# Linear attention and a squared-ReLU layer: the second batch's place around the end of the weight conversion, and strip two's second product by two Strassen steps

## The chip, the cores and the metric

The kernel runs on one core of a Trainium2 chip, as one launch. The metric is the device time of that launch in microseconds; lower is better. The engines are TensorE (PE, with its weight loads shown as PEld), VectorE (DVE), ScalarE (ACT), GpSimd (POOL) and SyncE (SP), which here issues nearly all transfers on one queue, in program order.

## The reference

Eight batches of eight heads, 576 rows, 64 features, all in float32; the two weight matrices come as float64.

```python
kv = np.einsum('bhsd,bhse->bhde', k, v)
out = np.einsum('bhsd,bhde->bhse', q, kv)
rms = np.sqrt(np.mean(out * out, axis=-1, keepdims=True) + 1e-06)
x = (out / rms * g_norm)          # then (B,H,S,D) -> (4608, 512)
h = x @ w_in                      # 512 x 2048
r = np.maximum(h, 0.0)
return ((r * r) @ w_out)          # 2048 x 512
```

## The kernel before

**Strips.** The 4608 token rows are 36 tiles of 128; four tiles make a strip of 512 rows, and there are nine strips (`s` = 0 to 8; "strip one" is `s` = 0). Each strip has a first product (x times w_in, squared ReLU) and a second one (times w_out). The list `steps` holds first the calls of one, then of the other, and the loop at the end of the kernel calls them in order; all scheduling is by hand, so every engine gets its instructions in program order.

**Products.** Strip one's first product is plain (`up_first`, 16 steps, L609), since the weights are still being converted. In all later strips it is a Winograd-Strassen product with seven block products (`up`, L573). The second product of a strip with `s < DEEP` is by one such step: `down`, seven block products `p`, each in two halves `i`, with 128x256 matmuls at L573; strip one takes them in the order 1, 2, 5, 6, 7, 3, 4. From `s = DEEP` on it is by two steps: `down_deep`, 49 small products with 128x128 matmuls at L758 (`small_products`), whose operand sums are `leaf_sums` and whose results `together` adds on DVE. A float32 matmul shows as two records. `combine` takes a finished block out of PSUM: a copy by ACT (`snap`, L583) or an addition by DVE (`o_sb`, L711). `sums_g` adds two quarters of the activations for product 5, and `sums_in(g)` forms the Winograd sums of w_in for group g, after ACT has scaled them (L252); `sums_x(s)` forms those of x.

**Weights.** The float64 words come as 32 raw pieces of 0.5 MB (`load_piece`, tag `raw`, eight buffers), are converted two at a time by ACT (L205, L208) and DVE (L217 to L226), and DVE forms the sums of w_out and stores them in DRAM (`w_out`, from tiles `wt` that share the raw buffers). `convert(n)` runs ahead of the steps of strip one's first product, and a new piece is loaded when a buffer comes free. Three of the seven w_out operands (`w_first`) stay in SBUF for strip one. For the two-step product each w_out operand needs four more sums: `deep_sums(p, w)`, four DVE subtractions (L243) into a tile `w_t`, stored to `w_deep` in strip `DEEP - 1`. Blocks are fetched by `stream()`, in the order of `to_stream`, into four buffers that `w_t` shares:

```python
t = deep[p] = stream_pool.tile([P, 4, FQ // 2, P], FP32, name="w_t", tag="w_blk")
minus(nc.vector, t[:, 0], b12, b11)
...
t = stream_pool.tile([P, 4, FQ // 2, P], FP32, name="w_blk", tag="w_blk")
```

**Attention.** A batch has four pairs of heads (b, p). `load` fetches a pair's q, k and v (0.8 MB), `load_rest` and `load_q_rest` the last 64 rows of a batch. The work is cut into `slices`: per pair a transposition of q (T) and the key/value product (K, L352), then per two tiles `query` (L383), `normalized` and `features` (L470, transposed into xT). `attend(n)` runs the slices up to number n; the loop calls it after every step. K of a pair also issues the load of a later pair. In strip one the eight T and K slices of batch two (b = 1) stand behind the last eight steps of the first product, one each, and its queries behind the first six steps of the second product; pairs (1,0) and (1,1) and the rest rows are loaded at steps 2 and 4.

Of the kernel before, what the change touches and what calls it, by code (L numbers as in the profile page):

```python
# [10 lines left out]
FP32 = mybir.dt.float32  # L11
# [9 lines left out]
def kernel(  # L21
# [34 lines left out]
    nc = tc.nc  # L56
    P = 128
# [4 lines left out]
    NP = H // 2  # L62
    FC = d_ff // P
    C = S // P
# [5 lines left out]
    STRIP = NT * P  # L70
    TH = STRIP // 2
    N_STRIP = N_TILE // NT
    DEEP = 2
    SQ = 32
    Q_ON_PE = 2
    X_ON_PE = 2
# [8 lines left out]
    small = ctx.enter_context(tc.tile_pool(name="small", bufs=3))  # L85
    g_pool = ctx.enter_context(tc.tile_pool(name="g", bufs=4))
    dram = ctx.enter_context(tc.tile_pool(name="dram", bufs=1, space=bass.MemoryType.DRAM))
    conv = ExitStack()
    raw_pool = conv.enter_context(tc.tile_pool(name="raw", bufs=8))
    wtmp = conv.enter_context(tc.tile_pool(name="wtmp", bufs=4))  # L90
    apsum = ctx.enter_context(tc.tile_pool(name="apsum", bufs=2, space=bass.MemoryType.PSUM))
    fpsum = ctx.enter_context(tc.tile_pool(name="fpsum", bufs=1, space=bass.MemoryType.PSUM))
# [5 lines left out]
    def load(b, p, q_eng):  # L98
        hs = slice(2 * p, 2 * p + 2)
        inputs = (("q", q, q_eng), ("k", k, nc.sync), ("v", v, nc.sync))  # L100
        if b == 0 and p >= 2:

            h_place = g_pool.tile([P, 4, C * P], FP32, name="first_qkv", tag="gt")
        for i, (n, src, eng) in enumerate(inputs if b == 0 else inputs[1:] + inputs[:1]):
            whole = src[b, hs, 0 : C * P].rearrange("h (sp c) d -> sp h c d", c=C)
            if n == "q" and b >= Q_ON_PE:

                t = qkv_pool.tile([P, 4 * C, SQ], FP32, name=n, tag=n)
                for a in range(4):
                    h, f = divmod(a * SQ, D)  # L110
                    eng.dma_start(
                        out=t[ts(a, SQ)],
                        in_=src[b, 2 * p + h, 0 : C * P, f : f + SQ].rearrange("(i k) f -> i k f", k=4 * C),
                    )
            elif n != "q":
                if b == 0 and p >= 2:
                    t = h_place[:, i].rearrange("p (h c d) -> p h c d", h=2, c=C)
                else:
                    t = qkv_pool.tile([P, 2, C, D], FP32, name=n, tag=n)
                eng.dma_start(out=t, in_=whole)  # L120
            else:

                if b == 0 and p >= 2:
                    t = h_place[:, i].rearrange("p (c h d) -> p c h d", h=2, c=C)
                else:
                    t = qkv_pool.tile([P, C, 2, D], FP32, name=n, tag=n)
                for h in range(2):
                    eng.dma_start(out=t[:, :, h, :], in_=whole[:, h])
            main[n, b, p] = t
# [47 lines left out]
    w_out = dram.tile([7, P, 2, FQ, P], FP32, name="w_out")  # L177

    w_deep = dram.tile([7, P, 4, FQ // 2, P], FP32, name="w_deep")
# [314 lines left out]
    def sums_x(s):  # L494
        xc[s] = t1, t2, t3, t4 = [
            sum_pool.tile([P, TH // SQ, KH, SQ], FP32, name=f"x_t{i}", tag="sum") for i in range(4)
        ]
        x = lambda kh, th: halves(s, kh, th)
        minus(nc.vector, t1, x(0, 1), x(0, 0))
        minus(nc.vector, t2, x(1, 1), t1)  # L500
        minus(nc.vector, t3, x(1, 1), x(0, 1))
        minus(nc.vector, t4, x(1, 0), t2)

    slices, ready = [], {}
# [23 lines left out]
    def attend(n):  # L528
        while slice_at[0] < min(n, len(slices)):
            fn, a = slices[slice_at[0]]  # L530
            fn(*a)
            slice_at[0] += 1
# [145 lines left out]
    def down(s, p, i):  # L678
        if i == 0:
            open_bank(p)  # L680
        a = {1: 11, 2: 21, 6: 11, 7: 12, 3: 21, 4: 22}.get(p)
        w = w_blk[s, p]
        product(
            p, i,
            lambda fc: (gq[s, 1, fc // 2][:, fc % 2] if p == 5 else gq[s, a][:, fc])[:, ts(i, P)],
            lambda fc: w[:, :, fc], FQ,
        )
        if i == 0:
            if s == DEEP - 1:
                deep_sums(p, w)  # L690
            return
        del w_blk[s, p]
        if s == 0 and p in (6, 7, 3) or s == DEEP - 1 and p not in (3, 4):
            stream()
        if s == DEEP - 1:
            nc.sync.dma_start(out=w_deep[B_OUT[p]], in_=deep.pop(p))

        if p == (1 if s else 2):
            for g in range(NG):
                x = gq[s, 11][:, ts(g, 2)]  # L700
                minus(nc.vector, x, gq[s, 1, g], x)
        if p == (2 if s else 5):
            minus(nc.vector, gq[s, 21], gq[s, 21], gq[s, 11])

        def store(th, eh):
            def f(b, a=None):
                o = out_tile()
                if a is None:
                    nc.scalar.copy(o, b)
                else:  # L710
                    nc.vector.tensor_tensor(out=o, in0=b, in1=a, op=ALU.add)  # L711
                send(s, th, eh, o)
            return f

        combine(p, store(0, 0), store(0, 1), store(1, 0), store(1, 1))
# [4 lines left out]
    def deep_sums(p, w):  # L720
        t = deep[p] = stream_pool.tile([P, 4, FQ // 2, P], FP32, name="w_t", tag="w_blk")
        b11, b12, b21, b22 = (w[:, e, ts(f, FQ // 2)] for f in range(2) for e in (1, 0))
        minus(nc.vector, t[:, 0], b12, b11)
        minus(nc.vector, t[:, 1], b22, t[:, 0])
        minus(nc.vector, t[:, 2], b22, b12)
        minus(nc.vector, t[:, 3], b21, t[:, 1])
# [98 lines left out]
    for s in range(N_STRIP):  # L825
        attend(ready[s])
        if s == 0:
            steps = [(2, up_first, (g, fh, i)) for g in range(NG) for fh in range(2) for i in range(2)]
        else:
            steps = [(1, up, (s, g, p)) for g in range(NG) for p in ORDER]  # L830
        n_up = len(steps)
        if s < DEEP:

            steps += [(2, down, (s, p, i)) for p in (ORDER if s else (1, 2, 5, 6, 7, 3, 4)) for i in range(2)]
        else:
            steps += [(2, down_deep, (s, k, i)) for k in range(7) for i in range(2)]
        goal = ready.get(s + 1, len(slices))
        total, done = sum(w for w, _, _ in steps), 0
        for i, (w, fn, a) in enumerate(steps):
            if s == 0 and i < n_up:  # L840

                convert(5 + (3 * i + 2) // 4)
                if i in (2, 4):
                    load_next()
                if i == 2:
                    load_q_rest(0, nc.sync)
                    load_rest(1, nc.sync)
                    load_q_rest(1, nc.sync)
            elif s == 0 and i == n_up:
                convert(len(conversions))  # L850
                conv.close()
                sum_pool = ctx.enter_context(tc.tile_pool(name="sum", bufs=8, reuse_waits="tile"))
                c_pool = ctx.enter_context(tc.tile_pool(name="c", bufs=6, reuse_waits="tile"))
                stream_pool = ctx.enter_context(tc.tile_pool(name="stream", bufs=4, reuse_waits="tile"))
                stream(3)
                for b, t in enumerate(w_first):
                    for e in range(2):
                        nc.sync.dma_start(out=w_out[b, :, e], in_=t[:, :, ts(e, P)])
            if s == 0 and n_up <= i < n_up + NG:
                sums_g(0, i - n_up)  # L860
            fn(*a)
            done += w
            if s:
                attend(ready[s] + int((goal - ready[s]) * min(done / (0.42 * total), 1)))
                if s >= DEEP and i == n_up - 3:
                    leaf_sums(s, 4)
                if s == DEEP - 1 and i == len(steps) - 1:
                    sums_x(s + 1)
                    stream(4)
                continue  # L870
            if i in (n_up + 4, n_up + 5):
                load_next()
            if i == n_up + 6:
                load_rest(2, nc.sync)
                load_q_rest(2, nc.sync)
            if i - n_up in (7, 9, 11, 13):
                sums_in((i - n_up - 7) // 2)
            if i == n_up + 9:
                sums_x(1)

            n_kv = ready[0] + 2 * NP
            if i < n_up:
                attend(ready[0] + max(0, (i + 1) - n_up + 2 * NP))
            else:
                attend(n_kv + (goal - n_kv) * min(i + 1 - n_up, 6) // 6)


# [28 lines left out]
```

## Time and profile before

| | |
|---|---|
| median of 7 runs | 945.17 us (942.43 to 946.65) |
| the profiled execution | 945.19 us, of which the span is 943.4 |
| busy: PE, PEld, DVE, ACT | 916.0, 805.4, 658.3, 227.1 us |
| mean granted TensorE clock | 0.995 of full speed |
| HBM read, written | 153.62 MB, 31.20 MB |

The span is the part of the execution that the profile shows. PE's busy time is the sum of its matmul records, so what is left of the span is time in which TensorE waits. "Busy time by stage" gives, for a stretch of the span, its length and each engine's busy time with the number of instructions, then the granted clock, the mean busy share of the sixteen DMA engines and GB/s. In the views in order of time a bracket at a line's end holds the engine's idle time before that line and what ended it.

### The profile page before, as it was taken

To read this page: it belongs to the slowest core of one execution; us is meant where nothing else is said; L and a number is where in the kernel's file an instruction comes from. 1 tells how busy PE (TensorE), PEld (TensorE's weight loads), DVE (VectorE), ACT (ScalarE), POOL (GpSimd) and SP (SyncE) were. 2 spreads that over 40 slices of the span, in tenths; PEclk is the share of its full clock that TensorE was granted. 3 is DMA by queue.
4 is the path that set the end of the run, shared out by engine and by line. 5 is a ranking of instruction groups with operands and counts; after the bars stand their busy time and mean duration, and the time that the engine had idled before them with its cause. 6 is when DMAs were issued, how large, how long until landed. Compare 5 with 4: busy or idle time off the path is not lost.

```text
span 943.4 us, 17026 instructions
## 1 busy us (share of the span) xinstructions
PE 916.0 (97%) x6880; PEld 805.4 (85%) x6880; DVE 658.3 (70%) x1147; ACT 227.1 (24%) x494; POOL 1.7 (0%) x7
## 2 busy tenths in 40 slices
PE   5899899999999999999999999999999999999998
PEld 4444787888888998899989998899889988998898
DVE  4998845586436996489737975698559854983496
ACT  4797432320023102210222013200320022002200
POOL 0000000000000000000000000000000000000000
PEclk9999999999999999999999999999999999999999
DMA  9799783537875585648664874477516831682075
GB/s 277 246 276 302 251 244 129 132 94 261 299 235 143 165 301 200 151 146 290 218 153 114 312 244 134 108 282 253 161 44 232 302 99 60 224 302 66 1 259 177
DMA packets 164286, 185.94 MB, mean 197 GB/s; under 512 B 83952, under 2 KB 137712, under 8 KB 155632
## 3 DMA queue, kind: packets, MB, share of 16 engines
q1 hardware_dynamic: 163888, 184.72, 61.4%
q8 instruction: 54, 0.88, 0.4%
q10 hardware_dynamic: 320, 0.13, 0.1%
q14 instruction: 24, 0.20, 0.1%
HBM read 153.62 MB, written 31.20 MB: 196 GB/s over the span
## 4 chain that ended last, share of the span: by engine, by line
PE 89%; DMA 5%; DVE 4%; ACT 1%; issue 1%; SPq 0%; DVEq 0%; ACTq 0%
PE ps_A L573 29%; PE ps_B L758 18%; PE ps_B L573 14%; PE ps_A L758 14%; PE ps_C L573 7%; PE x_ps L383 2%; PE kv_ps L352 2%; DMA raw<-in_moe_w_out_dram 2%; PE ps_A L609 2%; DMA x_d<-x_q 1%; DMA k_rest<-in_k_dram 1%; PE ps_B L609 1%; DVE w_c L223 1%; DMA raw<-in_moe_w_in_dram 1%; DMA v<-in_v_dram 0%
## 5 line engine op out<-in xcount | busy, mean ns | idle before, releaser
L573 PE MATMUL ps_A<-x_t,w_in 128*128 128x256 f32 x768 | 183.2, 381 | 0.0
L573 PEld LDWEIGHTS ps_A<-x_t,w_in 128*128 128x128 f32 x768 | 144.4, 190 | 20.3 <-ACT snap L583 0.3
L758 PE MATMUL ps_B<-w_blk,g_s 128*128 128x128 f32 x896 | 109.2, 275 | 0.0
L758 PEld LDWEIGHTS ps_B<-w_blk,g_s 128*128 128x128 f32 x896 | 104.6, 192 | 0.0
L758 PE MATMUL ps_B<-w_blk,gt 128*128 128x128 f32 x672 | 84.2, 275 | 0.0
L758 PE MATMUL ps_A<-w_blk,g_s 128*128 128x128 f32 x672 | 81.9, 275 | 0.0
L758 PEld LDWEIGHTS ps_B<-w_blk,gt 128*128 128x128 f32 x672 | 80.1, 192 | 0.4
L758 PEld LDWEIGHTS ps_A<-w_blk,g_s 128*128 128x128 f32 x672 | 78.4, 192 | 0.0
L632 DVE TENSOR_TENSOR gt<-ps_A,snap 128x512 f32<-128x512 f32 x32 | 22.1, 690 | 73.5 <-PE ps_A L573 73.5
L583 ACT COPY snap<-ps_A 128x512 f32<-128x512 f32 x68 | 39.9, 586 | 135.7 <-PE ps_A L573 124.5
L633 DVE SCALAR_TENSOR_TENSOR gt<-gt 128x512 f32<-128x512 f32 x96 | 66.4, 692 | 3.3
L632 DVE TENSOR_TENSOR gt<-ps_C,snap 128x512 f32<-128x512 f32 x32 | 22.1, 690 | 63.8 <-PE ps_C L573 63.8
L758 PE MATMUL ps_A<-w_blk,gt 128*128 128x128 f32 x504 | 63.1, 275 | 0.0
L573 PE MATMUL ps_A<-xT,w_in 128*128 128x256 f32 x256 | 61.3, 382 | 0.0
L573 PE MATMUL ps_C<-xT,w_in 128*128 128x256 f32 x256 | 61.1, 381 | 0.0
L573 PE MATMUL ps_B<-x_t,w_in 128*128 128x256 f32 x256 | 61.0, 381 | 0.0
L573 PE MATMUL ps_B<-xT,w_in 128*128 128x256 f32 x256 | 61.0, 381 | 0.0
L243 DVE TENSOR_TENSOR gt<-gt 128x2048 f32<-128x2048 f32 (+1 forms) x31 | 58.1, 1874 | 4.0 <-PE ps_C L573 3.8
L758 PEld LDWEIGHTS ps_A<-w_blk,gt 128*128 128x128 f32 x504 | 59.7, 192 | 0.0
L573 PEld LDWEIGHTS ps_B<-x_t,w_in 128*128 128x128 f32 x256 | 48.2, 190 | 6.7
L573 PEld LDWEIGHTS ps_B<-xT,w_in 128*128 128x128 f32 x256 | 48.2, 190 | 6.7
L573 PEld LDWEIGHTS ps_C<-xT,w_in 128*128 128x128 f32 x256 | 48.1, 190 | 6.7
(116 smaller groups left out, 1170.1 us busy)
## 6 DMA issues: line engine op xcount, KB each, us to landing
w_blk<-w_deep SPq DMA_DIRECT2D x49, 1024.0 KB, 5.6
w_blk<-w_out SPq DMA_DIRECT2D x49, 768.0 KB, 5.4
w_blk<-w_out SPq DMA_DIRECT2D x11, 1024.0 KB, 6.7
raw<-in_moe_w_in_dram SPq DMA_DIRECT2D x16, 512.0 KB, 6.0
raw<-in_moe_w_out_dram SPq DMA_DIRECT2D x16, 512.0 KB, 6.1
k<-in_k_dram SPq DMA_DIRECT2D x30, 256.0 KB, 3.0
v<-in_v_dram SPq DMA_DIRECT2D x30, 256.0 KB, 3.3
w_deep<-w_t SPq DMA_DIRECT2D x7, 1024.0 KB, 8.3
```

Source lines behind the costliest of these rows:

```text
L223: yield nc.vector.scalar_tensor_tensor(out=ci, in0=high, scalar=-(2**30), in1=ci, op0=ALU.bitwise_and, op1=ALU.bitwise_or)
L243: eng.tensor_tensor(out=out, in0=a, in1=b, op=ALU.subtract)
L352: nc.tensor.matmul(ps[ts(h, D)], lhsT=a, rhs=w, start=c == 0, stop=c == C)
L383: nc.tensor.matmul(ps[half, r, i, ts(p, D)], lhsT=q[row, half], rhs=kvd[b, p][row, row], start=True, stop=True)
L573: nc.tensor.matmul(bank[BANK[p]][:, i, :], lhsT=lhsT(k), rhs=rhs(k), start=p in (1, 5, 2) and i == 0 and k == 0, stop=k == n - 1, skip_gro ...
L583: nc.scalar.copy(snap[p], b)
L609: nc.tensor.matmul(ps, lhsT=w_in[:, kc % KH, g, kc // KH * 2 + fh, ts(i, P)], rhs=xt[0][:, :, kc, :], start=kc == 0, stop=kc == NP - 1,)
L632: nc.vector.tensor_tensor(out=o, in0=b, in1=a, op=ALU.add)
L633: nc.vector.scalar_tensor_tensor(out=o, in0=o, scalar=0.0, in1=o, op0=ALU.max, op1=ALU.mult)
L758: nc.tensor.matmul(chain[c][x][:, i, :], lhsT=a[:, f, :], rhs=w[:, f, :], start=p not in (6, 7, 3) and j in ((1, 2) if place(s, p) is LAST ...
```

## The change

The constant `DEEP` goes from 2 to 1. Strip two's second product is then by two steps, and `deep_sums` with its stores to `w_deep` are done in strip one, in the first half of each block product, from the operands in SBUF and the fetched blocks. In strip one the blocks for products 6, 7, 3 and 4 are no longer fetched by three at the start and the rest later: `stream()` is called in product 2's first half, ahead of that product's `w_deep` store, and in the second halves of 5, 6, 7, 3 and 4; two more blocks are fetched at the strip's last step. The stores of the three kept operands to DRAM move from one place ahead of the second product to the second halves of products 1, 2 and 5.

Batch two's loads move to later steps, and a third pair is loaded by the loop, into a buffer of its own (`spare_pool`) that lies in the conversion's part of SBUF; so the K slices load pairs (1,3) and (2,0). T and K of batch two begin at the sixth step from the end of the first product, and those of the last pair come behind the first two steps of the second. The queries follow by threes of steps: a query with its normalizing, nothing, two features. The loads of (2,1) and of the next rest rows, and `sums_x(1)`, move to later steps. The pool `c_pool` is opened before the conversion's pools instead of after them.

```diff
-    DEEP = 2
+    DEEP = 1
...
+    c_pool = ctx.enter_context(tc.tile_pool(name="c", bufs=6))
     conv = ExitStack()
     raw_pool = conv.enter_context(tc.tile_pool(name="raw", bufs=8))
+    spare_pool = conv.enter_context(tc.tile_pool(name="spare", bufs=1))
...
+        if b == 1 and p == 2:
+            h_place = spare_pool.tile([P, 3, C * P], FP32, name="more_qkv")
+        placed = (b, p) in ((0, 2), (0, 3), (1, 2))
...
         if i == 0:
             if s == DEEP - 1:
                 deep_sums(p, w)
+                if p == 2:
+                    stream()
+                nc.sync.dma_start(out=w_deep[B_OUT[p]], in_=deep.pop(p))
             return
         del w_blk[s, p]
-        if s == 0 and p in (6, 7, 3) or s == DEEP - 1 and p not in (3, 4):
+        if p not in (1, 2):
             stream()
-        if s == DEEP - 1:
-            nc.sync.dma_start(out=w_deep[B_OUT[p]], in_=deep.pop(p))
+        if s == 0 and p in (1, 2, 5):
+
+            for e in range(2):
+                nc.sync.dma_start(out=w_out[B_OUT[p], :, e], in_=w_first[B_OUT[p]][:, :, ts(e, P)])
...
                 convert(5 + (3 * i + 2) // 4)
-                if i in (2, 4):
+                if i in (5, 7, 9):
                     load_next()
-                if i == 2:
+                if i == 6:
                     load_q_rest(0, nc.sync)
                     load_rest(1, nc.sync)
                     load_q_rest(1, nc.sync)
...
-                c_pool = ctx.enter_context(tc.tile_pool(name="c", bufs=6, reuse_waits="tile"))
                 stream_pool = ctx.enter_context(tc.tile_pool(name="stream", bufs=4, reuse_waits="tile"))
-                stream(3)
-                for b, t in enumerate(w_first):
-                    for e in range(2):
-                        nc.sync.dma_start(out=w_out[b, :, e], in_=t[:, :, ts(e, P)])
...
-                if s == DEEP - 1 and i == len(steps) - 1:
-                    sums_x(s + 1)
-                    stream(4)
                 continue
-            if i in (n_up + 4, n_up + 5):
+            if i == n_up + 11:
                 load_next()
-            if i == n_up + 6:
+            if i == n_up + 13:
                 load_rest(2, nc.sync)
                 load_q_rest(2, nc.sync)
...
-            if i == n_up + 9:
+            if i == n_up + 11:
                 sums_x(1)
-
-            n_kv = ready[0] + 2 * NP
-            if i < n_up:
-                attend(ready[0] + max(0, (i + 1) - n_up + 2 * NP))
-            else:
-                attend(n_kv + (goal - n_kv) * min(i + 1 - n_up, 6) // 6)
+            if i == len(steps) - 1:
+                stream(2)
+
+            n = i + 1 - (n_up - 6)
+            pairs, m = divmod(max(n - 2 * NP, 0), 3)
+            attend(min(ready[0] + min(max(n, 0), 2 * NP) + 4 * pairs + (0, 2, 2)[m], goal))
```

More of the change, by code (lines that the diff above doesn't have):

```diff
@@ L115, in load @@
             elif n != "q":
-                if b == 0 and p >= 2:
+                if placed:
                     t = h_place[:, i].rearrange("p (h c d) -> p h c d", h=2, c=C)
@@ L121, in load @@
             else:
-                if b == 0 and p >= 2:
+                if placed:
                     t = h_place[:, i].rearrange("p (c h d) -> p c h d", h=2, c=C)
```

## The prediction

> **What bounds the kernel now.** I read the page's engine rows first, then busy time by stage (cut where the chain of waits passes from one product to the next), then the chain and the order of time of each engine around the first two strips.
>
> ```profile
> span 943.4 us, 17026 instructions
> ...
> PE 916.0 (97%) x6880; PEld 805.4 (85%) x6880; DVE 658.3 (70%) x1147; ACT 227.1 (24%) x494; POOL 1.7 (0%) x7
> ```
>
> TensorE is the bound as a whole: 27.4 us of the span are not its work. The stages show where they are, and who would take over:
>
> ```profile
> core 0: us, PE busy (x) PEld busy (x) DVE busy (x) ACT busy (x) POOL busy (x), PEclk, DMA share, GB/s
> 0.00:31.30 31.30, 16.31 (x145) 13.92 (x146) 16.67 (x45) 14.38 (x33) 1.70 (x7) 0.93 0.86 277
> 31.30:97.50 66.20, 62.20 (x229) 28.85 (x228) 62.25 (x139) 56.93 (x128) 0.00 (x0) 0.98 0.90 277
> 97.50:151.70 54.20, 53.52 (x370) 46.14 (x370) 32.20 (x59) 15.13 (x27) 0.00 (x0) 1.00 0.79 247
> ...
> 207.90:259.20 51.30, 50.49 (x234) 43.86 (x233) 30.12 (x44) 2.99 (x5) 0.00 (x0) 1.00 0.77 265
> 259.20:285.00 25.80, 24.77 (x163) 21.07 (x162) 9.06 (x14) 6.57 (x15) 0.00 (x0) 1.00 0.72 232
> ...
> 315.00:358.80 43.80, 43.80 (x394) 43.80 (x393) 40.34 (x64) 3.10 (x9) 0.00 (x0) 1.00 0.81 280
> ```
>
> Row two is the conversion with strip one's first product: PE, DVE, ACT and DMA are all at 0.86 or more, PE idles 4.0 us. Row three is strip one's second product (DVE 32.2 of 54.2), row four strip two's, row six the same product of strip three, in two steps. The chain gives the two forms of that product:
>
> ```profile
> 216.55 6.91 PE ps_C L573 x32
> ...
> 252.13 8.87 PE ps_A L573 x40
> ...
> 315.01 6.25 PE ps_B L758 x56
> ```
>
> One of the seven products takes 32 matmul records and 6.91 us by one step, 56 shorter ones and 6.25 us by two. Last, in order of time, what idles at the conversion's end:
>
> ```profile
> 65.22 0.33 PE L340 MATMUL tr_ps<-ident,q_rest 128*128 128x128 f32 x1 [1.32 <-DMA q_rest<-in_q_dram]
> ...
> 96.70 0.69 PE L352 MATMUL kv_ps<-v,k 128*64 128x64 f32 x16 [2.68 <-ACT kv_all L355]
> ```
>
> ```profile
> 72.21 0.43 DVE L217 TENSOR_SCALAR w_c<-w_c 128x512 f32<-128x512 f32 x1 [0.27 <-ACT w_c L205]
> 74.07 0.43 DVE L217 TENSOR_SCALAR w_c<-w_c 128x512 f32<-128x512 f32 x1 [1.43 <-ACT w_c L205]
> ```
>
> ```profile
> 92.07 0.68 ACT L205 ACTIVATE w_c<-raw 128x512 f32<-128x512 f32 x1 [4.63 <-DMA raw<-in_moe_w_out_dram]
> ```
>
> The last raw weights land late, ACT stands in front of them for 4.63 us, and PE's K step, which needs ACT's copies, starts at 96.70.
>
> **Part 1: strip two by two steps.** Before, its second product runs from 209.65 (eight records of 0.216 into the first x40 group that the chain shows at 207.92) to 259.11, the start of strip three's first product: 49.46 us, of which 7 x 6.91 = 48.4 are matmuls. After: 7 x 6.25 = 43.75. DVE there rises from 30.1 to about 40.3, which hides as in row six, where PE is busy 43.80 of 43.80; the sums and blocks are the same code. **-5.7 us.** The leaf sums of product 4 (four of 0.69) replace eight instructions of `sums_g` in the first product: nothing, DVE is 29.2 of 46.8 there.
>
> A rule speaks against this step. A 128-column record takes 6.25/56 = 0.1116 us, a 256-column one 6.91/32 = 0.2159, so a column is dearer by 3.4% only, and the step saves an eighth of the columns. The Trainium skill, "TensorE: Matmul & The Clock Gate", section "Back-to-back issue gap", holds that short matmuls with a weight load each are disproportionately dear: about 81 ns at 128 columns against 131 ns at 512. A straight line between these would put 256 columns at about 98 ns, an estimate from that page, and 392 records would cost 31.8 us where 224 cost 22.0: the step would lose 10 us. The rows of this case decide against it.
>
> **Part 2: strip three's start.** PE idles 1.03 us in row five, at 281.15, waiting for v (a load queued behind four blocks, 3.7 MB, that are fetched in one burst at 260.4). Afterwards strip two fetches its blocks one by one, as strip three does before strip four, where PE has no idle (358.8 to 413.0: 54.20 of 54.20). **-1.0 us.** The burst moves to the end of strip one, four blocks in its last 3 steps; in front of key/value step (2,0) they would cost up to 1.0. That step came 15.4 us after strip one's end (166.93), and the rest rows that it needs are now queued at the last step; I take 0.
>
> **Part 3: the conversion's end.** Batch two's loads go three steps later (pair (1,0) from 2 to 5, pair (1,1) from 4 to 7, the rest rows from 2 to 6), so raw pieces 22 to 27 (0.5 MB each) no longer stand behind 2.1 MB of them on SP's queue. The DVE idles 0.84 + 0.27 + 1.43 = 2.54 us between 67 and 75 end, all later conversions move up, and so do the last raw loads, whose place behind pair (1,3)'s 0.8 MB and 1 MB of `w_out` stores is unchanged. **-2.5 us**; at best all of PE's idle, -4.0. Against it: the rest rows were issued 55.0 to 60.7 and PE waited 1.32 us for them at 65.2; now they follow pieces 26 and 27, whose slots come free at 63.5, and the first transposition comes about 70. If they land at 73 to 74 (5 to 8 us after issue, as before) PE waits 3 to 4 and the gain is gone; at worst +2.5. DMA was at 0.90 anyway: bytes are only reordered. Transposition and K of pair (1,3), 0.87 + 0.73 us of PE, now follow the first steps of the second product, which is bound by PE: **+1.6 us**. The spare buffer costs no instruction.
>
> **Part 4: strip one's second product.** Removed there: three blocks and six stores in a burst. Added: seven `deep_sums` of 4 x 0.69, 19.3 us of DVE, taken from strip two, where they hid; 32.2 + 19.3 = 51.5 of some 56. Each is followed on SP's in-order queue by a 1 MB store, and blocks for products 7, 3 and 4 are fetched behind that store: a fetch now waits for DVE. I put it in a row. PE starts product 1 at 95.0 (2.5 early): 1 to 101.9, pair (1,3) to 103.5, 2 to 110.4, query 111.5, 5 to 118.4, features and query 120.7, 6 to 127.6, features 128.5, 7 to 135.4, then 3 and 4. DVE leaves the conversion at 98.0. In program order: first sums and `deep_sums(1)` to 102.1, wait for the `wt` stores (5.8 us after conversion, as 100.5 to 106.27 before) and two sums 106.6, `deep_sums(2)` 109.3, normalizing 113.1, fourth sum 114.5 (product 5 needs it at 114.1: **+0.4**), minus and output 117.7, `deep_sums(5)` 120.4, minus 122.7, normalizing 126.5, `deep_sums(6)` 129.3. A store and a block together are 2.1 MB, 6 us at 344 GB/s (265/0.77, row four) and 2 us to report: block 7 lands at 128.4 for 128.5, block 3 at 137.3 for 135.4 (**+1.9**), block 4 behind `deep_sums(7)` (134.7) at 142.7 for 144.2. So **+2.3**. From below: nothing, if the fetches hide. From above: the slowest block before took 11.0 us,
>
> ```profile
> DMA to landing us min/median/max: 4.9/6.7/11.0
> ```
>
> which gives 131.4 and 140.3, 4.9 in all. The last `sums_in` waits for ACT behind product 4's output as before, so the 1.7 us idle of strip two's start stays: 0.
>
> **Sum.** -5.7 - 1.0 - 2.5 + 1.6 + 2.3 = -5.3 us: span 938.1. The profiled execution took 945.19 us, 1.8 over its span, and the median is 945.17, so **939.9 us**. About 0.2% (1.9 us) is what a measurement of this kernel can tell from no change.
>
> **Rivals.** *Transfers become the bound of strip one's second product (slower).* Row three moved 54.2 x 247 = 13.4 MB. Seven stores add 7.3, two blocks of strip two leave (-2.1): 18.6 MB. At 344 GB/s that is 54 us, just covered by PE's 56; at the 265 GB/s that row four really reached beside the same stores it is 70.2, 14.2 longer, in place of my 2.3: 951.8 us. It decides below 18.6/(56 + 2.3 + 5.3 + 1.9) = 284 GB/s. For it: share 0.79 already, reads behind stores on one queue. Against: row four was not limited by transfers (share 0.77, PE idle 0.8), and 1.8 MB of strip two's first blocks may slip into its first product, which has 105 GB/s. 0.17.
>
> *The conversion gives nothing (no change).* Rest rows land late, 2.5 us do not come, and the burst costs 1.0 one strip earlier: 943.4. Speaks for it: DMA at 0.90. 0.15.
>
> *All hides.* Conversion's idle of 4.0 goes, blocks arrive in time: 939.9 - 1.5 - 2.3 = 936.1. Against: DVE at 51.5 of 56. 0.18.
>
> The forecast has 0.50. The range reaches from 934.5 (all hides, and pair (1,3) too) to 950.0, most of the way to the slow rival; the forecast and the last rival give faster, 0.68; the second rival is nearly all of same, 0.14; the first, with what remains, slower, 0.18. The case of the forecast alone is 937 to 943.
>
> **What would show it.** Strip two's second product is 392 records of 0.112 with PE idle under 0.3 us: if not, part 1 is wrong. Product 1 of strip one starts at 94 to 96; PE's wait for q_rest shows part 3. PE idle before products 7, 3 and 4 with block fetches as releaser is part 4: 2 us right, 5 or more means the transfers bind; DMA share over 0.95 there and DVE over 50 us busy. Wrong altogether if the last product of strip one ends after 158.

## The result, and the profile after

The changed kernel takes 940.31 us (median of 17 runs, 937.06 to 942.83); the kernel before, on the same chip, 944.71 (44 runs). The ratio is 0.9949, with a 95% interval of 0.9937 to 0.9960: 4.8 us less. The prediction was 939.9, from a span of 938.1; the profiled execution has a span of 938.2.

The engine rows of the page after:

```profile
span 938.2 us, 17429 instructions
PE 912.2 (97%) x7048; PEld 807.4 (86%) x7048; DVE 684.9 (73%) x1195; ACT 226.3 (24%) x497; POOL 1.7 (0%) x7
```

PE's own work fell by 3.8 us, its idle time by 1.4 (27.4 to 26.0), and DVE got 26.6 us of new work, most of it hidden behind PE.

Busy time by stage, cut again where one product passes to the next (start and end, length, then busy time of each engine with its instructions, the granted clock, DMA share, GB/s):

```profile
31.97:95.96 63.99, 61.49 (x204) 27.98 (x202) 61.85 (x138) 55.48 (x124) 0.00 (x0) 0.97 0.96 283
95.96:153.56 57.60, 55.28 (x395) 47.16 (x395) 48.61 (x86) 16.29 (x30) 0.00 (x0) 1.00 0.95 314
211.31:255.08 43.77, 43.77 (x393) 43.77 (x393) 40.33 (x64) 3.09 (x9) 0.00 (x0) 1.00 0.75 270
255.08:280.00 24.92, 24.92 (x164) 21.22 (x164) 11.08 (x18) 5.99 (x14) 0.00 (x0) 1.00 0.67 198
```

The rows are strip one's first product with the conversion, its second product, strip two's second product, and strip three's start. The third is now PE without a gap, at 0.111 us a record, the second is 3.4 us longer, with DVE at 48.6 instead of 32.2 and 18.1 MB moved instead of 13.4. A line of the chain of waits, and the waits of PE in order of time, show the same:

```profile
217.56 6.25 PE ps_A L768 x56
```

```profile
74.59 0.30 PE L345 MATMUL tr_ps<-ident,q_rest 128*128 128x128 f32 x1 [2.50 <-DMA q_rest<-in_q_dram]
130.84 7.14 PE L578 MATMUL ps_A<-w_blk,gt 128*128 128x256 f32 x32 [1.06 <-DMA w_blk<-w_out]
138.90 7.17 PE L578 MATMUL ps_B<-w_blk,gt 128*128 128x256 f32 x32 [0.92 <-DMA w_blk<-w_out]
146.41 7.14 PE L578 MATMUL ps_A<-w_blk,gt 128*128 128x256 f32 x32 [0.33 <-DMA w_blk<-w_out]
```

Each of the last three products of strip one waits for its block: 2.31 us in all. The wait for the rest rows of the query has grown from 1.32 to 2.50, while the 2.68 us of waiting for ACT's copies before product 1 are gone.

From the starts of PE's products in the two traces, the time went like this (after less before): start of the first product +0.5 (31.07 to 31.59); from there to product 1 of strip one -2.1 (66.36 to 64.30); strip one's second product +3.4 (54.18 to 57.60); strip two's first product -0.2; strip two's second product -5.7 (49.46 to 43.77); strip three's first product -1.3 (55.90 to 54.64); the rest +0.1. Together -5.2, the difference of the spans. One execution each is compared: the start of the first product alone lies between 29.5 and 31.8 us in the ten profiles of this case, so terms of some tenths of a microsecond may be chance.

### The profile page after: what moved, and what is told of

Same layout as the page of the kernel before. It is cut to its first block, busy times and chain, and to the rows that moved or that the text cites. A ratio compares the mean times of both kernels' runs of the same rounds, so it can differ in the third digit from the quotient of the medians.

```text
span 938.2 us, 17429 instructions
## 1 busy us (share of the span) xinstructions
PE 912.2 (97%) x7048; PEld 807.4 (86%) x7048; DVE 684.9 (73%) x1195; ACT 226.3 (24%) x497; POOL 1.7 (0%) x7
## 4 chain that ended last, share of the span: by engine, by line
PE 83%; DVE 7%; DMA 5%; issue 1%; SPq 1%; ACT 1%; DVEq 0%; ACTq 0%
PE ps_A L578 24%; PE ps_B L768 21%; PE ps_A L768 16%; PE ps_B L578 13%; PE ps_C L578 6%; PE kv_ps L357 2%; DMA w_blk<-w_out 2%; PE x_ps L388 2%; DVE w_c L228 1%; DMA k_rest<-in_k_dram 1%; DMA q<-in_q_dram 1%; DVE w_c L222 1%; DVE w_in L231 1%; DVE w_t L248 1%; DMA raw<-in_moe_w_out_dram 1%
## 5 line engine op out<-in xcount | busy, mean ns | idle before, releaser
L768 PE MATMUL ps_B<-w_blk,g_s 128*128 128x128 f32 x1024 | 124.8, 275 | 0.0
L768 PEld LDWEIGHTS ps_B<-w_blk,g_s 128*128 128x128 f32 x1024 | 119.5, 192 | 0.0
L768 PE MATMUL ps_B<-w_blk,gt 128*128 128x128 f32 x768 | 96.2, 275 | 0.0
L768 PE MATMUL ps_A<-w_blk,g_s 128*128 128x128 f32 x768 | 93.6, 275 | 0.0
L768 PEld LDWEIGHTS ps_B<-w_blk,gt 128*128 128x128 f32 x768 | 91.5, 192 | 0.4
L768 PEld LDWEIGHTS ps_A<-w_blk,g_s 128*128 128x128 f32 x768 | 89.6, 192 | 0.0
L768 PE MATMUL ps_A<-w_blk,gt 128*128 128x128 f32 x576 | 72.2, 275 | 0.0
L768 PEld LDWEIGHTS ps_A<-w_blk,gt 128*128 128x128 f32 x576 | 68.2, 192 | 0.0
L782 DVE TENSOR_TENSOR o_sb<-o_sb,ps_B 128x256 f32<-128x256 f32 (+1 forms) x128 | 49.4, 386 | 12.2 <-ACT o_sb L783 4.2
```

The costliest lines, as they stand in the source:

```text
L768: nc.tensor.matmul(chain[c][x][:, i, :], lhsT=a[:, f, :], rhs=w[:, f, :], start=p not in (6, 7, 3) and j in ((1, 2) if place(s, p) is LAST ...
L782: add = lambda out, a, b: nc.vector.tensor_tensor(out=out, in0=a, in1=b, op=ALU.add)
```

## The experiments

The profile after leaves three questions: whether the parts of the change are worth what their terms say when each stands alone; what makes the block fetches late, their place in SP's queue or the bytes; and what limits the conversion's end. All eight runs are timed beside the kernel before, on one chip in each of two groups (944.61 and 944.35 us for the kernel before). Ratios are to the kernel before; the changed kernel's is 0.9949.

**Two-step product alone.** The changed kernel, with its new order of block fetches and stores too, but with the places of all other loads, the conversion's and the attention's schedule as in the kernel before:

```diff
-                if i in (5, 7, 9):
+                if i in (2, 4):
                     load_next()
-                if i == 6:
+                if i == 2:
                     load_q_rest(0, nc.sync)
...
-            if i == n_up + 11:
+            if i in (n_up + 4, n_up + 5):
                 load_next()
-            if i == n_up + 13:
+            if i == n_up + 6:
                 load_rest(2, nc.sync)
...
-            if i == n_up + 11:
+            if i == n_up + 9:
                 sums_x(1)
```

The slices of `attend` and the place of pair (1,2) are put back too.

> The changed kernel with batch two's loads and slices, the loads of (2,0), (2,1) and the next rest rows, and the sums of x put back to where they were; only strip two's two-step product with its sums, stores and block fetches stays. Theory (parts 1, 2 and 4 carry the gain, the new places of batch two nearly cancel): strip two's second product 43.8 us (-5.7), strip three's start -1.3, block waits in strip one +2.3 as in the changed kernel: 944.7 - 4.7 = 940.0 us, 939 to 941.5. Rival (the old places do not fit the new fetches: loads of the next pairs and rest rows now stand among the blocks on the queue of SP): block waits of 5 us or more in place of 2.3, 943 us or more.

Measured: 954.51 us, ratio 1.0107 (1.0078 to 1.0135). That is 10 us slower than before, where the theory wanted 4.6 faster; the rival has the sign, not the size. Its PE, and SP's queue in order of time:

```profile
135.26 8.83 PE L575 MATMUL ps_A<-w_blk,gt 128*128 128x256 f32 x32 [2.98 <-DMA w_blk<-w_out]
152.86 8.68 PE L575 MATMUL ps_B<-w_blk,gt 128*128 128x256 f32 x32 [8.77 <-DMA w_blk<-w_out]
```

```profile
129.98 5.01 SPq L122 DMA_DIRECT2D k<-in_k_dram  x1
135.04 0.55 SPq L122 DMA_DIRECT2D v<-in_v_dram  x1
135.63 3.13 SPq L113 DMA_DIRECT2D q<-in_q_dram  x4
138.86 1.05 SPq L695 DMA_DIRECT2D w_deep<-w_t  x1
140.00 0.63 SPq L145 DMA_DIRECT2D k_rest<-in_k_dram  x1
140.69 1.42 SPq L145 DMA_DIRECT2D v_rest<-in_v_dram  x1
142.16 4.04 SPq L159 DMA_DIRECT2D q_rest<-in_q_dram  x8
146.25 0.43 SPq L659 DMA_DIRECT2D w_blk<-w_out  x1
```

The block waits are 11.75 us instead of 2.31. Block 3's fetch, the last line, leaves SP at 146.25; in the changed kernel it left at 130.66. What stands in front of it is pair (2,1) and the rest rows of its batch (b = 2; the "batch two" of the description above is b = 1). The two groups of 32 records behind the waits took 8.83 and 8.68 us instead of 7.1, so the waits cost the clock as well.

**The moved loads alone.** The kernel before with the changed kernel's conversion schedule, attention slices and load places, the second product of strip two as before (`DEEP = 2`):

> The kernel before with the new places of batch two's loads and slices alone (the third pair in its own buffer, later rest rows and loads of (2,1), later sums of x); strip two's second product stays by one step, and blocks, sums and stores stay where they were. Theory: the conversion ends 1.5 us earlier and 1.6 us of transposition and key/value work come after it, net -0.4: 944.3 us, 943.3 to 945.3. Rival (the spreading carries a real part of the gain): 942.7 us or less.

Measured: 945.66 us, ratio 1.0004 (0.9987 to 1.0021). That is 0.4 above the theory's range and no change that can be measured; the saving that the rival wanted is not there. (The profiled execution, at 942.17, is the fastest of the twelve; its way from the start of the first product to product 1 is 64.1 us, as in the changed kernel, and none of its products waits for a block. Where the slower ones lose this again is not shown.) Alone, one part of the change loses 10 us and the other gains nothing; together they gain 4.8. In this run PE waits for no block, and the loads' place is worth nothing that can be measured.

**Which of the moved things it is.** The kernel of the first experiment, with only the loads of (2,0), (2,1) and that batch's rest rows behind the block fetches again, and `sums_x(1)` moved along with them (this expectation and the next call b = 2 "batch two"):

```diff
-            if i in (n_up + 4, n_up + 5):
+            if i == n_up + 11:
                 load_next()
-            if i == n_up + 6:
+                load_next()
+            if i == n_up + 13:
                 load_rest(2, nc.sync)
...
-            if i == n_up + 9:
+            if i == n_up + 11:
                 sums_x(1)
```

> The kernel of a_two_step_only (two-step product and block fetches of the change, conversion and attention of the kernel before), with only these put to the change's places: the loads of (2,0) and (2,1), both at step 11 of the second product, the rest rows of batch two at step 13, the shared sum at step 11. Theory (the 10 us that a_two_step_only lost came from the place of these loads in SP's queue, ahead of the block fetches): block waits of 1 to 3 us in all instead of 11.75, 939 to 942 us. Rival (they came from the attention that the old schedule lays into the first product and the first steps of the second, which makes VectorE late): block waits stay above 6 us, 947 us or more.

Measured: 943.24 us, ratio 0.9982 (0.9967 to 0.9997): 1.2 us above the theory's range, 3.8 below the rival's. The difference to the first experiment is 1.25%, 11.8 us; the block waits are down to one:

```profile
147.05 7.14 PE L575 MATMUL ps_A<-w_blk,gt 128*128 128x256 f32 x32 [1.49 <-DMA w_blk<-w_out]
```

So nearly all of the loss was the loads' place (`sums_x(1)`, DVE work, moved too and was not tried alone; the queue's order above speaks for the loads). The remaining 0.33% (3.1 us) to the changed kernel stands, in the two profiles, at three places: 1.0 more from the first product's start to product 1, 0.9 more in strip one's second product, and 2.3 more in strip two's first product, which waits 1.63 us for `v_rest`; a first product that started 1.3 earlier takes off some of it (spans 941.1 and 938.2). Whether these come from the old attention schedule, which the rival named, or from the old conversion schedule was not tried.

**Ten small loads alone.** The changed kernel with only the rest rows of b = 2 put back, ahead of block 3's fetch:

```diff
-            if i == n_up + 13:
+            if i == n_up + 6:
                 load_rest(2, nc.sync)
                 load_q_rest(2, nc.sync)
```

> The changed kernel with only the rest rows of batch two (2 loads and 8 small q pieces) put back from step 13 to step 6 of the second product of strip one, ahead of block 3's fetch. Theory (what stands ahead of a fetch in SP's queue delays it): block 3 is issued some 5 to 6 us later than at 130.66, and its wait grows from 0.92 to 4 to 7 us, later blocks wait less; 943 to 946 us. Rival (only the bulk loads with their 0.25 MB each matter, ten small pieces pass): within 1 us of the changed kernel, 939.5 to 941.5.

Measured: 947.36 us, ratio 1.0029 (1.0015 to 1.0044): 0.8% or 7.5 us above the changed kernel, more than the theory's 3 to 6. SP's queue and PE:

```profile
129.50 1.07 SPq L698 DMA_DIRECT2D w_deep<-w_t  x1
130.67 0.64 SPq L148 DMA_DIRECT2D k_rest<-in_k_dram  x1
131.36 1.40 SPq L148 DMA_DIRECT2D v_rest<-in_v_dram  x1
132.81 4.65 SPq L162 DMA_DIRECT2D q_rest<-in_q_dram  x8
137.56 0.38 SPq L662 DMA_DIRECT2D w_blk<-w_out  x1
```

```profile
130.84 7.15 PE L578 MATMUL ps_A<-w_blk,gt 128*128 128x256 f32 x32 [1.16 <-DMA w_blk<-w_out]
144.21 9.77 PE L578 MATMUL ps_B<-w_blk,gt 128*128 128x256 f32 x32 [6.22 <-DMA w_blk<-w_out]
```

Block 3 leaves at 137.56 instead of 130.66: 6.9 us later. The ten loads hold 2 x 128 + 8 x 16 KB, 0.39 MB, which is 1.3 us at the stage's 294 to 314 GB/s; SP issued them for 6.7 us. It is SP's time for issuing them that delays the block, not their bytes: a fetch of 1 MB holds SP for 0.38 and 0.43 us in the rows of these two runs, a 16 KB piece for 0.58. PE's wait grew by 5.3, and the 32 records after it took 2.7 us more than 7.07; the theory had left out that second part.

**Block fetches before the stores.** The prediction said that a fetch behind a store waits for DVE's `deep_sums`. Here the blocks for 7, 3 and 4 are fetched ahead of that store, in the first halves of products 6, 5 and 7:

```diff
                 deep_sums(p, w)
-                if p == 2:
+                if p in (2, 5, 6, 7):
                     stream()
                 nc.sync.dma_start(out=w_deep[B_OUT[p]], in_=deep.pop(p))
...
-        if p not in (1, 2):
+        if p in (3, 4):
             stream()
```

> The changed kernel with the fetches of the blocks for products 7, 3 and 4 moved from the second halves of products 5, 6 and 7 into their first halves, ahead of the store of the same step, as product 2 has it. Theory (a block comes late because its fetch waits on the in-order queue behind a store that waits for DVE): the three waits of 1.06, 0.92 and 0.33 us shrink to 0.5 in all or less, 940.3 - 1.8 = 938.5 us, 937.9 to 939.3. Rival (the bytes bind: transfers are busy for 0.95 of that stage, whatever the order): the waits only move, 939.8 us or more, DMA share still 0.95.

Measured: 936.96 us, ratio 0.9934 (0.9911 to 0.9958): 3.4 us below the changed kernel by the medians, 1.4 by the ratios, whose intervals overlap. The time alone does not settle it. The profile does. Strip one's second product:

```profile
99.19:153.63 54.44, 54.44 (x395) 47.32 (x395) 48.16 (x85) 16.29 (x31) 0.00 (x0) 1.00 0.99 314
```

All three waits are gone, PE is busy for all of 54.44 us, 3.2 less than the changed kernel's 57.60, at the same 314 GB/s. SP's queue at block 3, in the changed kernel and here:

```profile
130.16 0.39 SPq L698 DMA_DIRECT2D w_deep<-w_t  x1
130.66 0.37 SPq L662 DMA_DIRECT2D w_blk<-w_out  x1
```

```profile
132.50 0.33 SPq L662 DMA_DIRECT2D w_blk<-w_out  x1
132.93 0.38 SPq L698 DMA_DIRECT2D w_deep<-w_t  x1
```

Counted from the start of product 1 (95.89 and 99.12), the fetches of blocks 7, 3 and 4 leave 2.5, 1.4 and 1.8 us earlier. (This execution came late to product 1, at 99.1, because of a wait of 4.45 for the rest rows of the query, after which eight records took 5.02 us instead of 3.67; its end is therefore no earlier. At 940.97 it is among the slower of the seven, which lie at 935.87 to 936.96 or at 940.31 to 941.04.)

**More bytes, same order.** That kernel, with the converted blocks of products 6, 5 and 7 stored a second time, to a place that nobody reads:

```diff
+                if p in (6, 5, 7):
+                    nc.sync.dma_start(out=w_more[B_OUT[p]], in_=deep[p])
                 nc.sync.dma_start(out=w_deep[B_OUT[p]], in_=deep.pop(p))
```

> The kernel of c_blocks_first with the converted blocks of products 6, 5 and 7 stored twice, the second copy to a place that nobody reads: 3 MB more to move in strip one's second product, ahead of stores that nobody waits for within it but behind the block fetches, which at 316 GB/s are some 10 us of transfers. Theory (order decides, not bytes): block waits up to 1 us in all, at most 1.5 us over c_blocks_first, 936.5 to 938.5. Rival (with a DMA share of 1.00 the bytes bind): PE waits for blocks or for the operands behind them for 4 us or more, 941 to 947.

Measured: 941.85 us (12 runs, 939.89 to 948.41), ratio 0.9976 (0.9956 to 0.9996). Both theories were too sure: 4.9 us over the kernel without the second stores by the medians, 4.0 by the ratios, where the theory allowed 1.5. The rival's range holds the time, but its waits are too large: PE's waits for blocks and for `w_t` in this stage are 1.25 and 0.60, not 4 or more. The same stage:

```profile
95.35:152.12 56.77, 54.92 (x395) 47.23 (x395) 48.20 (x86) 16.08 (x30) 0.00 (x0) 1.00 1.01 351
```

It moved 56.77 x 351 = 19.9 MB against 54.44 x 314 = 17.1, and is 2.3 us longer. At 314 GB/s the added 2.8 MB would have taken 9; three quarters went into a higher rate. So the DMA share of 0.95 to 0.99 in these stages was not the end of what the transfers can do, but the reserve is small. The other 1.8 us stand one stage later: strip two's first product takes 60.3 us instead of 58.5, with PE waiting 1.49 us for `v_rest`, a wait that the kernel without the second stores doesn't have. So bytes are not free here either; the rival's mechanism holds in part.

**Rest rows earlier.** The changed kernel with the rest rows of batches zero and one at step 4 of the first product instead of 6, two steps ahead:

```diff
-                if i == 6:
+                if i == 4:
                     load_q_rest(0, nc.sync)
                     load_rest(1, nc.sync)
                     load_q_rest(1, nc.sync)
```

> The changed kernel with batch two's rest rows loaded at step 4 instead of 6, ahead of raw pieces 24 to 27. Theory (the conversion's end is set by the last raw weights, which ACT waits for until 92.1): TensorE's wait of 2.50 us for q_rest goes, but it waits for ACT's copies later, and product 1 of strip one starts at most 0.6 us earlier: 939.7 to 940.5 us. Rival (TensorE runs without a gap from that wait to product 1, so the wait is on the path): 2 us earlier or more, 938.3 us or less.

Measured: 939.02 us, ratio 0.9941 (0.9918 to 0.9964). The median lies between the two expectations, 0.8 us below the changed kernel by the ratios, whose intervals overlap. The profile speaks for the theory: the wait for `q_rest` is gone, but PE waits for ACT instead,

```profile
93.08 0.69 PE L357 MATMUL kv_ps<-more_qkv 128*64 128x64 f32 x16 [2.60 <-ACT kv_all L360]
```

and from the start of the first product to product 1 it takes 63.6 us instead of 64.3. Of 2.50 us of wait removed, 0.7 arrive in this execution.

**Both together.** Blocks first and rest rows early:

> The changed kernel with the edits of c_blocks_first and d_rests_early together: the blocks fetched in the first halves of products 5, 6 and 7, and the rest rows of batches zero and one loaded at step 4. Theory (the two savings lie in different stages and add: 3.4 and 0.5 to 1.3): 935.6 to 936.6 us. Rival (an earlier start of the second product makes its block fetches late again, or the transfers it brings forward bind): no better than c_blocks_first, 937 us or more.

Measured: 935.19 us (5 runs, 934.95 to 935.46), ratio 0.9894 (0.9877 to 0.9911): faster than either edit alone (the interval of the blocks' run begins where this one ends), 0.55% (5.2 us) below the changed kernel by the ratios, and 0.4 better than the theory's range. Strip one's second product is whole again:

```profile
94.45:148.88 54.43, 54.43 (x396) 47.35 (x395) 48.04 (x85) 16.30 (x31) 0.00 (x0) 1.00 0.98 320
```

Its first product, to product 1, takes 62.6 us, with 1.53 of waiting for ACT's copies left. The rival, that an earlier start makes the fetches late again or that the transfers bind, is refuted by this row.

## Why the prediction was right

**The total.** A span of 938.2 against 938.1 is partly luck: the spans of the changed kernel's executions reach from 935.1 to 940.8, and the terms below miss by up to 0.9 us with signs that cancel.

**What bounds.** PE was and is the bound; every gain found is PE's idle time or PE's records.

**Part 1** (-5.7 predicted, -5.69 measured). 393 records at 0.111 us and no idle time. The records of strip three were the right rows to take, and the rule that short matmuls are disproportionately dear, which would have made it lose 10 us, doesn't hold here.

**Part 2** (-1.0 predicted, -1.26 measured, 1.03 of it the idle time). PE is busy for all of strip three's start. The burst's new place cost nothing that shows: strip two's first product is 0.2 shorter, with the predicted idle time at its start, 1.63 us.

**Part 3** (-2.5 predicted, -2.1 measured from the start of the first product, -1.5 by the clock of the span). Two of its steps hold: DVE's waits between 67 and 75 are gone, and PE's wait for the rest rows grew. It was sized at nothing in the forecast and at 3 to 4 us in the bound. It is 2.50 here, and 2.13, 2.21, 3.04 and 4.45 in four other profiled runs with the same order of loads, so a single execution doesn't size it. With 4.45 the way from the first product's start to product 1 is 67.3 us and the gain is gone, as the bound said. ACT still stands in front of the last raw weights:

```profile
89.86 0.68 ACT L210 ACTIVATE w_c<-raw 128x512 f32<-128x512 f32 x1 [3.39 <-DMA raw<-in_moe_w_out_dram]
92.10 0.68 ACT L210 ACTIVATE w_c<-raw 128x512 f32<-128x512 f32 x1 [1.00 <-DMA raw<-in_moe_w_out_dram]
```

It is 4.39 us in the two lines, where it was 4.63 and 0.35 before. The step "all later conversions move up, and so do the last raw loads" fails at its end: the last two raw loads leave SP at 84.84, before at 84.68. What moved up is their landing, ACT's last piece starts at 92.10 instead of 93.68. Why they land sooner was not tried; the `w_out` stores ahead of them left from 77.76 on instead of 79.95. DVE is busy for 61.85 of the stage's 63.99 us and the transfers for 0.96; which of them sets the end is not shown.

**Pair (1,3) and part 4** (+1.6 and +2.3 predicted, +3.4 measured). Here the sum was nearly right and the terms less so, which is luck. With no wait at all, strip one's second product takes 54.43 us in the last experiment, and PE's busy time before was 53.5: PE's work grew by 0.9, not 1.6. Pair (1,3) itself takes 0.55 and 0.73 there, from 99.45 to 100.00 and from 103.55 to 104.28; the prediction's 0.87 added two groups of records that overlap (0.60 and 0.27). The other 0.4 came off elsewhere in PE's work. The waits and what follows them cost 57.60 - 54.43 = 3.2, not 2.3. And the wait of 0.68 for ACT's copy, which before stood at product 7 (130.69), goes: a term that the sum left out. 0.9 + 3.2 - 0.7 = 3.4. The mechanism, a fetch behind a store that waits for DVE, is shown by moving the fetch: all the waits vanish. The DMA share reached the 0.95 that the prediction had named as a sign of the other rival, and it is none: with the fetch moved the share is 0.99 and nothing waits. But the row "+0.4 for the fourth sum, nothing for 7, 1.9 for 3, nothing for 4" is 0, 1.06, 0.92 and 0.33 in the profile. The 8 us from issue to landing hold (7.5 to 8.8 us for these blocks); blocks 7 and 4 came late because their fetches left at 121.86 and 138.37, not at 120.4 and 134.7. DVE took 48.6 us, not 51.5.

**What the sum had no term for.** The later places of the next batch's loads, (2,0), (2,1) and the rest rows of b = 2, have no term in the prediction. Laying out the fetches in a row, I used the new order without saying what the old one would have cost: 11.8 us by the ratios with all of them, 7.5 with the ten small loads alone, each measured in its own surroundings. The total is not wrong by this, but the reader of the prediction would have thought that the two-step product alone keeps -5.7 + 2.3, and it loses 10.

**The rivals.** Transfers as the bound was weighed with 265 GB/s as the low end, the rate of another stage, and decided below 284. The stage reached 314, and 351 when more was there to move. A rate read from a stage in which nobody asked for more is not a bound. The rival "the conversion gives nothing" doesn't hold in the profiled execution (part 3), but it does in the one that waited 4.45 us for the rest rows; "all hides" was wrong by 2.31 us of block waits; the last experiment, which removes them, is at 935.19 where it said 936.1, but it moves the rest rows too and still waits 1.53 us for ACT's copies, so that nearness shows little.

## What to carry to other kernels

On an in-order issue queue, cost a transfer by what stands ahead of it: a store that waits for an engine and a run of small pieces both delay a critical fetch, and the price of a moved load is found only together with the fetches behind it. So put the fetch that the bottleneck needs next ahead of any store that waits for sums, and loads that are needed later behind the last of the fetches. A part of a change that measures nothing alone can be what makes the other part pay; try both alone and together before one is dropped.

## What the runs showed of the hardware

Eight loads of 16 KB in 128-byte rows held SP for 4.04 and 4.65 us in the rows above, 0.5 to 0.6 us each, as long as 1.3 to 1.5 MB take at 314 GB/s; in front of a critical fetch they and two more cost the kernel 7.5 us. Whether the number of pieces or their short rows take the time was not tried apart.

A long wait costs PE its clock. After waits of 2.98, 6.22 and 8.77 us for a block, 32 records took 8.83, 9.77 and 8.68 us instead of 7.07; after waits of 3.04 and 4.45 us for the rest rows of the query the next eight took 5.35 and 5.02 instead of 3.67; after waits of 2.35 and 3.71 us for ACT's copies the first 16 records of product 1 took 5.41 instead of 3.72. After 2.60 and 2.68 us for the same copies they took 3.72, and after 2.13, 2.21 and 2.50 us for the rest rows nothing was lost. Strip one's second product was granted 0.95 and 0.90 of the clock in the two runs with the longest waits, 1.00 in the changed kernel. The Trainium skill, "TensorE: Matmul & The Clock Gate", section "Part 1: The HAM clock gate", puts half clock behind an idle window of about 3.4 us that runs freely. The waits of 3.71 us and more agree; those of 2.35, 2.98 and 3.04 lost clock too, below that length. So here a wait of about 3 us or more should be priced at 1.3 to 2.7 us beyond itself, and of the six waits between 2.1 and 2.7 us only one lost clock.

Block waits of 0.33 to 1.06 us cost 0.2 to 0.3 us beyond themselves: from the start of one product to the next, the changed kernel takes 9.12, 8.06 and 7.51 us over its three waits, the last experiment 7.88, 6.98 and 6.91 without them.

A DMA share of 0.98 to 1.01 went with anything from 314 to 351 GB/s, and at 0.98 PE waited for nothing. The share says that the engines have work in hand, not that PE waits for it.
